# Gate tiles in 64-row matmuls, column sums by a DMA transpose, one fold matmul fewer, and a weight block loaded in two pieces

## The chip, the cores and the metric

One core of a Trainium2 chip. The time is the device time of one execution in microseconds (us), taken from several executions; all runs told of here are in the fast state. The executions of one kernel spread over some 0.6 to 0.9 us (before: 144.69 to 145.32 in one set of six, 144.84 to 145.74 in another of eleven), so effects of 0.1 us are read from traces, not from times. A ratio is the mean time of one kernel's fast runs over that of the other's fast runs in the same rounds, so it isn't quite the ratio of the medians that stand beside it.

In the profile lines PE is TensorE's matmuls, PEld its weight loads, DVE VectorE, ACT ScalarE, POOL GpSimd, SP SyncE (which here only issues DMAs: loads, stores and transposes). L708 is line 708 of that kernel's file, so the same code has other numbers in the changed kernel: L708 there is L709, L742 is L743, L972 is L973, L620 is L621, L679 is L680, L712 is L713. "Block 0" and "block 1" are the first 384 rows of the first two column blocks of `w1`; to "land" is to be complete in SBUF. The "first gate" and the "second gate" (nothing to do with the gate tiles) are two places where TensorE can be made to wait: before H4, for block 1, and near 15 us, for a PSUM bank.

## The reference

```python
xn = layernorm(A_x)                               # 2048 tokens, D = 448
q, k, v = split_heads(xn @ wqkv)                  # 16 heads of 28
pq, pk = phi(q), phi(k)                           # phi(t) = (t + 1 if t > 0 else exp(t)) + 1e-6
kv  = einsum("bhsd,bhse->bhde", pk, v)
z   = einsum("bhsd->bhd", pk)                     # column sums of pk over all tokens
num = einsum("bhqd,bhde->bhqe", pq, kv)
den = einsum("bhqd,bhd->bhq", pq, z) + 1e-6
s   = merge_heads(num / den) @ wo
h   = relu(xn @ w1 + b1) ** 2                     # F = 1792
g   = silu(h @ w2 + b2)
return A_x + s * g
```

## The kernel before

A small scheduler in the file takes a list of operations. TensorE's and SP's order is the order of the list; the order on VectorE, ScalarE and GpSimd is chosen by a simulation. All engines run their lists in order.

The first weight block and the first feed-forward units. `w1` comes in blocks of 512 columns: its first 384 rows (three chunks of 128) in one load, the last 64 rows in two small ones. H0 to H6 are the first seven units, done first for tiles 0 and 1 (part 0), then for tiles 2 and 3 (part 1):

```python
load_x(0, 1); load_x(1, 2); load_x(2, 4)          # SP
...                                               # small loads on ScalarE's queue
load_w1(0, "sp", "act")                           # block 0: 384 KB on SP
load_w1(1, "sp", "sp")                            # block 1: 384 KB and 2 x 32 KB on SP
load_x(4, 8)                                      # 448 KB
load_k("sp", w_qkv, A_wqkv, "wk", D, 2 * D)
...
for c in range(3):
    pe_part([H0[i] for i in range(4)], 0, (c,))   # 12 matmuls: chunk c of block 0 and of xT
pe_part([H0[i] for i in range(4, 6)], 0)          # H4, H5: 6 matmuls, need block 1
piece, evac = x_transpose0(2, [(0, 1, 2, 3)])     # 8 TensorE transposes of tiles 2, 3
...
pe_part([H0[6]], 0)
for c in range(3):
    pe_part([H0[i] for i in range(4)], 1, (c,))   # the "second halves": 12 matmuls
```

The pieces that the rest of the change touches:

```python
def gg(si):                                       # one gate tile: 14 matmuls of all 128 rows
    for fi in range(NF):
        e.matmul(ps(b)[:, 0:D], r2[:, fi, si*P:(si+1)*P], w_2[:, fi, :], start=(fi == 0), ...)
    ...                                           # VectorE adds b2
def z_cols():                                     # column sums: zb holds the sum over the token tiles
    for c in range(5):
        e.matmul(ps(b)[:, c:c+1], zb[:, k:k+P], ones[:, :], ...)
    ...                                           # VectorE multiplies by the head mask -> zsb
def fold_wo(c):                                   # c = 3: two matmuls of 64 columns each
    ...
def gg_part(si, lo, hi):                          # last tile, by halves: bias by a matmul, then 14
    e.matmul(ps(b)[:, 0:w], ident[:, :], b2b[:, lo:hi], start=True, stop=False)
    ...
```

The order after the first stage: the units of the second 512 tokens, the gate tiles 0 to 3, the units of the third and fourth 512 tokens, the token sums, `z_cols`, the denominators, the folds, the other gate tiles and the output.

## Time and profile before

| | |
|---|---|
| time | 144.98 us median (144.69 to 145.32, 6 runs) |
| TensorE busy | 138.0 of 143.1 us |
| VectorE, ScalarE, GpSimd busy | 65%, 54%, 23% |
| first matmul of H0 | 6.86 us |
| last matmul ends | 139.53 us |

TensorE sets the time from 6.9 us on. The chain's pieces are shown in the prediction.

### The profile page before, as it was taken

The page shows a single profiled execution, that of the slowest core. Times are in us where ns is not written, and L with a number is a line of the kernel's source. Part 1 is how long each engine was busy: PE and PEld are TensorE (multiplying, and loading weights), DVE is VectorE, ACT ScalarE, POOL GpSimd, SP SyncE. Part 2 cuts the span into 40 slices and gives each one's busy share as a digit, 9 for nine tenths or more (in the row PEclk, how much of TensorE's full clock was granted, in tenths as well). Part 3 has the DMA queues.
Part 4 walks back from the last instruction along what each step waited for, and adds up shares of the span by engine and source line. Part 5 has one row for each costly group of instructions (what it writes and reads, how often), then busy time and mean ns, then how long its engine had stood idle before and what let it go on. Part 6 is the DMA issues. An engine that isn't in the chain of part 4 may idle for free.

```text
span 143.1 us, 2830 instructions
## 1 busy us (share of the span) xinstructions
PE 138.0 (96%) x1114; PEld 72.4 (51%) x1114; DVE 92.5 (65%) x212; ACT 77.1 (54%) x148; POOL 32.7 (23%) x50
## 2 busy tenths in 40 slices
PE   7799999999999999999999999999999999999990
PEld 7685444444455444444444455546455554554590
DVE  5869879899997156768999760003511793575661
ACT  3617897988877088888879761178312131100120
POOL 2114026254000117300560000000000000399900
PEclk9999999999999999999999999999999999999999
DMA  3977899970452400000000000001499200024341
GB/s 80 315 247 201 173 240 337 338 170 0 41 111 55 92 0 5 0 0 0 5 0 0 5 0 0 0 0 23 124 174 179 39 0 5 0 75 149 116 144 33
DMA packets 17008, 12.43 MB, mean 87 GB/s; under 512 B 7844, under 2 KB 16100, under 8 KB 16996
## 3 DMA queue, kind: packets, MB, share of 16 engines
q1 hardware_dynamic: 16416, 11.28, 29.8%
q10 hardware_dynamic: 580, 0.97, 3.5%
q8 instruction: 9, 0.15, 0.4%
q14 instruction: 3, 0.02, 0.1%
HBM read 8.78 MB, written 1.90 MB: 75 GB/s over the span
## 4 chain that ended last, share of the span: by engine, by line
PE 93%; DVE 2%; DMA 1%; ACT 1%; issue 0%
PE pb L972 28%; PE pb L712 27%; PE pb L620 7%; PE pb L781 6%; PE pb L646 6%; PE pb L1041 6%; PE pb L708 3%; PE pb L994 2%; DMA x_tok<-in_A_x_dram 1%; PE pb L1114 1%; PE pb L660 1%; PE pb L787 1%; PE pb L857 1%; DVE st L462 1%; PE pb L809 1%; PE pb L879 1%
## 5 line engine op out<-in xcount | busy, mean ns | idle before, releaser
L972 PE MATMUL pb<-w,r 128*128 128x448 bf16 x210 | 40.7, 353 | 0.0
L712 PE MATMUL pb<-xT,w 64*128 64x512 bf16 (+1 forms) x291 | 38.1, 376 | 0.0
L679 ACT ACTIVATE r<-pb,b1f 128x512 bf16<-128x512 f32 x54 | 33.7, 691 | 6.8 <-PE pb L712 6.8
L972 PEld LDWEIGHTS pb<-w,r 128*128 128x128 bf16 x210 | 20.2, 98 | 19.5 <-issue 0.8
L1014 ACT ACTIVATE gbuf<-gbuf 128x448 bf16<-128x448 bf16 x15 | 8.1, 571 | 28.4 <-DVE gbuf L981 24.2
L1030 POOL TENSOR_TENSOR obuf<-obuf,x_tok 128x448 bf16<-128x448 bf16 x12 | 12.1, 1044 | 49.4 <-DVE obuf L1024 49.4
L981 DVE TENSOR_TENSOR gbuf<-pb,b2b 128x448 bf16<-128x448 f32 x15 | 9.3, 620 | 20.5 <-PE pb L972 20.5
L712 PEld LDWEIGHTS pb<-xT,w 64*128 64x128 bf16 (+1 forms) x291 | 14.3, 94 | 16.4
L693 DVE TENSOR_TENSOR r<-r 128x512 bf16<-128x512 bf16 x37 | 18.3, 523 | 2.9 <-ACT r L679 2.9
L630 POOL TENSOR_TENSOR zacc<-zacc,pk 128x448 f32<-128x448 f32 x13 | 14.4, 1107 | 22.8 <-DVE pk L610 22.3
L620 PE MATMUL pb<-w_qkv,xT 64*128 64x448 bf16 x112 | 13.2, 349 | 0.0
L1024 DVE TENSOR_TENSOR obuf<-pb,gbuf 128x448 bf16<-128x448 f32 (+1 forms) x17 | 9.3, 591 | 4.0 <-PE pb L1041 2.4
L598 ACT ACTIVATE pk<-pb 128x448 bf16<-128x448 f32 x16 | 7.8, 541 | 7.4 <-PE pb L620 7.4
L694 ACT ACTIVATE r<-r 128x512 bf16<-128x512 bf16 x19 | 11.2, 634 | 0.0
L646 PE MATMUL pb<-xT,w_qkv 64*128 64x512 bf16 x84 | 11.0, 376 | 0.0
L462 DVE BATCH_NORM_STATS2 st<-x_tok 128x6 f32<-128x448 bf16 x16 | 9.3, 615 | 1.7 <-DMA x_tok<-in_A_x_dram 1.7
L712 PE MATMUL pb<-xT,w_1r 64*128 64x512 bf16 x56 | 10.3, 377 | 0.0
L610 DVE SCALAR_TENSOR_TENSOR pk<-pb,pk 128x448 bf16<-128x448 f32 x16 | 9.9, 623 | 0.5
L781 PE MATMUL pb<-pk,xn 128*128 128x448 bf16 x48 | 9.4, 352 | 0.0
L603 DVE TENSOR_SCALAR pk<-pk 128x448 bf16<-128x448 bf16 x16 | 6.2, 392 | 4.4 <-ACT pk L598 4.4
L620 PEld LDWEIGHTS pb<-w_qkv,xT 64*128 64x128 bf16 x112 | 5.4, 94 | 6.1 <-issue 0.4
L610 DVE SCALAR_TENSOR_TENSOR pqT<-pb,pqT 128x512 bf16<-128x512 f32 x12 | 8.2, 689 | 0.3
(87 smaller groups left out, 123.8 us busy)
## 6 DMA issues: line engine op xcount, KB each, us to landing
out_dram<-obuf SPq DMA_DIRECT2D x15, 112.0 KB, 1.7
w<-in_B_w_dram SPq DMA_DIRECT2D x1, 1568.0 KB, 9.3
x_tok<-in_A_x_dram SPq DMA_DIRECT2D x3, 448.0 KB, 4.7
w<-in_B_w_dram SPq DMA_DIRECT2D x3, 384.0 KB, 4.5
w_qkv<-in_A_wqkv_dram SPq DMA_DIRECT2D x3, 336.0 KB, 5.5
pk<-rden_rows ACTq DMA_DIRECT2D x6, 112.0 KB
pk<-rden_rows SPq DMA_DIRECT2D x5, 112.0 KB
w_o<-in_A_wo_dram SPq DMA_DIRECT2D x1, 392.0 KB, 8.8
```

Source lines behind the costliest of these rows:

```text
L462: op = add("dve", lambda e, _: e.bn_stats(st6[:, si, :], x_tok[:, si, :]), [("x", si)], [("st", si)], 0.58)
L610: lambda e, _: e.scalar_tensor_tensor(out=slot, in0=ps(buf)[:, 0:n], scalar=1.0 + 1e-6, in1=slot, op0=ALU.add, op1=ALU.max),
L620: return e.matmul(ps(b)[:, 0:D], xT[rw, si, c, :], w_qkv[rw, c, D : 2 * D], start=start, stop=stop)
L630: lambda e, _: e.tensor_tensor(out=o[:, 0:D], in0=pk[:, 0, :] if i == 1 else zacc[:, :], in1=pk[:, i, :], op=ALU.add),
L646: return e.matmul(ps(b)[:, 0:512], w_qkv[rw, c, m * P : (m + 1) * P], xT[rw, 4 * g : 4 * g + 4, c, :], start=start, stop=stop,)
L679: rl = lambda e, _: e.activation(out=slot, in_=ps(b)[:, 0:512], func=AF.Relu, bias=b1f[:, fi : fi + 1])
L693: return e.tensor_tensor(out=slot, in0=slot, in1=slot, op=ALU.mult)
L694: return e.activation(out=slot, in_=slot, func=AF.Square)
L712: return e.matmul(ps(b)[:, 0:512], lhs, xT[rw, 4 * g : 4 * g + 4, c, :], start=start, stop=stop, skip_group_check=not full,)
L781: last = e.matmul(ps(b)[:, 0:D], xn[:, si, c * P : (c + 1) * P], pk[:, si, :], start=(si == 0), stop=(si == NT - 1),)
L972: last = e.matmul(ps(b)[:, 0:D], r2[:, fi, si * P : (si + 1) * P], w_2[:, fi, :], start=(fi == 0), stop=(fi == NF - 1),)
L1030: lambda e, _: e.tensor_tensor(out=ob, in0=ob, in1=x_tok[:, si, lo:hi], op=ALU.add),
```

## The change

Its intent: take slots and changes of array form off TensorE, and let it start on the first chunk of `w1` before the others are there. The core of the diff, with cuts marked:

```diff
+            for c0, c1 in ((0, 1), (1, 3)) if p == 0 else ((0, 3),):      # load_w1
+                dma(eng, w_1[:, c0:c1, lo:hi], B_w1[c0*P : c1*P, lo:hi]..., [("w1", p, 0, c) for c in range(c0, c1)], ...)
...
-            need = {("xTp", 2 * part, k) for k in cs} | {u[1][0] for u in us}
+            need = {("xTp", 2 * part, k) for k in cs} | {u[1][0] + (k,) for u in us for k in cs}
...
         def z_cols():
-            ... five matmuls with a column of ones, one multiply
+            add("sp", lambda e, _: e.dma_start_transpose(zbT[:, :, :], zb[:, :]), ...)
+            add("dve", lambda e, _: e.tensor_reduce(out=zcol[:, :], in_=zbT[:, :, :], op=ALU.add, axis=X), ...)
+            ... two multiplies by the mask
...
         def fold_wo(c):
-                for o in range(1 if c < 3 else 2): ... 64-column halves for c = 3
+                for h in hs: e.matmul(ps(b)[:, 0:D], kvm[0:PD, h, c*P:(c+1)*P], w_o[0:PD, h, :], ...)
...
+        def gg4(t):                       # four gate tiles; two 64-row matmuls at a time
+            for i, pair in enumerate(((t, t+2), (t+1, t+3), (t+2, t), (t+3, t+1))):
+                for fi in range(NF):
+                    for h in (0, 1):
+                        e.matmul(ps(bufs[pair[h]])[:, 0:D], r2[half[h], fi, ...], w_2[half[h], fi, :], ...)
...
-        gg(0)
-        gg(1)
-        gg(2)
-        gg(3)
+        gg4(0)
...
-        gg_part(15, 0, 224)
+        gg_part(15, 0, 224, False)        # bias by VectorE instead of a matmul
```

The warm-up matmuls also read a constant instead of a tile that VectorE clears first, `kvm` is 512 wide, and the scheduler's estimate for the denominators is 0.88 us instead of 0.22.

More of the change, by code (lines that the diff above doesn't have):

```diff
@@ L312, in bass_recurrent_scan__linear_attn_block__dense_activation_squared_relu__prompt_kernel @@
         zmask = sb("zmask", [P, 5, 32], f32)
-        ones = sb("ones", [P, 1], bf)
-        wz = sb("wz", [P, P], bf)
+        wz = nc.const_aps.tensor(1.0, [P, P], bf)
         rsp = nc.dram_tensor("rden_rows", [NH, 2, 1024], bf)
@@ L336, in bass_recurrent_scan__linear_attn_block__dense_activation_squared_relu__prompt_kernel @@
         zb = sb("zb", [P, 512], bf)
+        zbT = sb("zbT", [P, 4, P], bf)
+        zcol = sb("zcol", [P, 4], f32)
         at = sb("at", [P, 4, D], bf)
@@ L339, in bass_recurrent_scan__linear_attn_block__dense_activation_squared_relu__prompt_kernel @@
         r2 = sb("r2", [P, NF, S], bf)
-        kvm = sb("kvm", [P, 4, D], bf)
+        kvm = sb("kvm", [P, 4, 512], bf)
         msb = at
@@ L373, in vset @@
             add("dve", lambda e, _: e.memset(ap, val), [name] if again else [], [name], dur)
-        vset(wz[:, :], 0.0, "wz")
-        pr.ops[-1].prio = -1e6
         vset(hmask[:, :], 1.0, "hmask", dur=0.15)
@@ L379, in bass_recurrent_scan__linear_attn_block__dense_activation_squared_relu__prompt_kernel @@
         vset(kvm[:, :, :], 0.0, "kvm", dur=1.0)
-        pool(lambda e, _: e.memset(ones[:, :], 1.0), ["ones"], dur=0.1)
         pool(lambda e, _: e.memset(eps6[:, :], 1e-6), ["eps6"], dur=0.1)
@@ L433, in load_w1 @@
             m = (hi - lo) // 2
-            dma(
-                eng, w_1[:, :, lo:hi], B_w1[0:384, lo:hi].rearrange("(c p) j -> p c j", p=P), [("w1", p, 0)],
-                768 * (hi - lo), reads,
-            )
+            for c0, c1 in ((0, 1), (1, 3)) if p == 0 else ((0, 3),):
+                dma(
+                    eng, w_1[:, c0:c1, lo:hi], B_w1[c0 * P : c1 * P, lo:hi].rearrange("(c p) j -> p c j", p=P),
+                    [("w1", p, 0, c) for c in range(c0, c1)], (c1 - c0) * 256 * (hi - lo), reads,
+                )
             load_w1r(p, eng2)
         w1names = lambda p: [("w1", p, i) for i in range(3)]
+        for p in range(4):
+            pr.alias(("w1", p, 0), [("w1", p, 0, c) for c in range(3)])
         load_x(0, 1)
@@ L816, in fold_wv @@
             add("pe", f, [("at", c) for c in range(4)] + wnames("wv"), [b], 16 * 0.057)
-            kd = free_ap(kvm[0:PD, 0:1, 0:PD], [[D + PD, 4], [1, PD]])
+            kd = free_ap(kvm[0:PD, 0:1, 0:PD], [[512 + PD, 4], [1, PD]])
             add(
@@ L825, in fold_wv @@
             )
+            add(
+                "dve", lambda e, _: e.tensor_copy(kvm[0:PD, 3, D:512], kvm[0:PD, 3, 384:D]), ["kvd"], ["kve"], 0.12
+            )
         def z_cols():
-            b = Buf("Z")
-            def f(e, _):
-                last = None
-                for c in range(5):
-                    k = min(c, 3) * P
-                    last = e.matmul(
-                        ps(b)[:, c : c + 1], zb[:, k : k + P], ones[:, :], start=(c == 0), stop=True,
-                        skip_group_check=True,
-                    )
-                return last
-            add("pe", f, ["zb", "zbd", "ones"], [b], 0.35)
-            z = lambda: free_ap(ps(b)[:, 0:5], [[1, 5], [0, 32]])
-            add(
-                "dve", lambda e, _: e.tensor_tensor(out=zsb[:, :, :], in0=z(), in1=zmask[:, :, :], op=ALU.mult),
-                [b, "zmask"], ["zsb"], 0.25,
-            )
+            add(
+                "sp", lambda e, _: e.dma_start_transpose(zbT[:, :, :], zb[:, :]),
+                ["zb", "zbd"], ["zbT"], 1.25, nbytes=P * 512 * 3,
+            ).fixed = 2.0
+            add(
+                "dve",
+                lambda e, _: e.tensor_reduce(
+                    out=zcol[:, :], in_=zbT[:, :, :], op=ALU.add, axis=mybir.AxisListType.X
+                ),
+                ["zbT"], ["zcol"], 0.6,
+            )
+            for i, n in ((0, 4), (4, 1)):
+                z = free_ap(zcol[:, min(i, 3) : min(i, 3) + n], [[1, n], [0, 32]])
+                add(
+                    "dve",
+                    lambda e, _, i=i, n=n, z=z: e.tensor_tensor(
+                        out=zsb[:, i : i + n, :], in0=z, in1=zmask[:, i : i + n, :], op=ALU.mult
+                    ),
+                    ["zcol", "zmask"], [("zsb", i)], 0.2,
+                )
         def fold_wo(c):
@@ L852, in f @@
                 last = None
-                for o in range(1 if c < 3 else 2):
-                    dst = ps(b)[:, 0:D] if c < 3 else ps(b)[64 * o : 64 * o + 64, 0:D]
-                    wd = P if c < 3 else 64
-                    for h in hs:
-                        last = e.matmul(
-                            dst, kvm[0:PD, h, c * P : c * P + wd], w_o[0:PD, h, :], start=(h == hs[0]),
-                            stop=(h == hs[-1]),
-                        )
+                for h in hs:
+                    lhs = kvm[0:PD, h, c * P : (c + 1) * P]
+                    last = e.matmul(ps(b)[:, 0:D], lhs, w_o[0:PD, h, :], start=(h == hs[0]), stop=(h == hs[-1]))
                 return last
-            add("pe", f, ["kvd", "kvm", "wo"], [b], 0.19 * len(hs) * (2 if c == 3 else 1))
+            add("pe", f, ["kvd", "kvm", "wo"] + (["kve"] if c == 3 else []), [b], 0.19 * len(hs))
             def ev(e, eng):
@@ L894, in den @@
                 "pe", f,
-                ["zsb"] + [("pq", g, c) for g in range(NG) for c in range(3)]
+                [("zsb", 0), ("zsb", 4)] + [("pq", g, c) for g in range(NG) for c in range(3)]
                 + [("pqx", u) for u in (0, 1)],
-                [denb], 0.22,
+                [denb], 0.88,
             ).mode = "col32"
@@ L985, in gg, with gg_bias, f, gg_part @@
             )
-        def gg_part(si, lo, hi):
+        def gg_bias(si, b):
+            add(
+                "dve",
+                lambda e, _: e.tensor_tensor(
+                    out=gbuf[:, si % NGB, :], in0=ps(b)[:, 0:D], in1=b2b[:, :], op=ALU.add
+                ),
+                [b, "b2b"], [("g", si % NGB)], 0.624,
+            )
+        def gg4(t):
+            half = (slice(0, 64), slice(64, 128))
+            bufs = {si: Buf("G") for si in range(t, t + 4)}
+            ops = []
+            for i, pair in enumerate(((t, t + 2), (t + 1, t + 3), (t + 2, t), (t + 3, t + 1))):
+                def f(e, _, pair=pair, i=i):
+                    last = None
+                    for fi in range(NF):
+                        for h in (0, 1):
+                            si = pair[h]
+                            last = e.matmul(
+                                ps(bufs[si])[:, 0:D], r2[half[h], fi, si * P : (si + 1) * P], w_2[half[h], fi, :],
+                                start=(i < 2 and fi == 0), stop=(i >= 2 and fi == NF - 1),
+                            )
+                    return last
+                banks = [bufs[si] for si in pair]
+                rd = [("r2", t // 4, fi) for fi in range(NF)] + ["w2"]
+                op = add("pe", f, rd + (banks if i >= 2 else []), banks, NF * MM(D))
+                op.mode = "row64"
+                ops.append(op)
+                if i >= 2:
+                    op.sync = ops[-3]
+                    for si in pair:
+                        gg_bias(si, bufs[si])
+        def gg_part(si, lo, hi, bias):
             b = Buf("G")
             w = hi - lo
+            gs = gbuf[:, si % NGB, lo:hi]
             def f(e, _):
-                last = e.matmul(ps(b)[:, 0:w], ident[:, :], b2b[:, lo:hi], start=True, stop=False)
+                last = e.matmul(ps(b)[:, 0:w], ident[:, :], b2b[:, lo:hi], start=True, stop=False) if bias else None
                 for fi in range(NF):
                     last = e.matmul(
-                        ps(b)[:, 0:w], r2[:, fi, si * P : (si + 1) * P], w_2[:, fi, lo:hi], start=False,
-                        stop=(fi == NF - 1),
+                        ps(b)[:, 0:w], r2[:, fi, si * P : (si + 1) * P], w_2[:, fi, lo:hi],
+                        start=(fi == 0 and not bias), stop=(fi == NF - 1),
                     )
@@ L1000, in gg_part @@
             rd = [("r2", si // 4, fi) for fi in range(NF)] + ["w2", "b2b", "ident"]
-            add("pe", f, rd, [b], (NF + 1) * max(MM(w), 0.098))
-            add(
-                "act",
-                lambda e, _: e.activation(out=gbuf[:, si % NGB, lo:hi], in_=ps(b)[:, 0:w], func=AF.Silu),
-                [b, "acts"], [("gh", lo)] + ([("g", si % NGB)] if lo == 0 else []), 0.2 + 0.00084 * w,
+            add("pe", f, rd, [b], (NF + bias) * max(MM(w), 0.098))
+            wr = [("gh", lo)] + ([("g", si % NGB)] if lo == 0 else [])
+            if not bias:
+                add(
+                    "dve",
+                    lambda e, _: e.tensor_tensor(out=gs, in0=ps(b)[:, 0:w], in1=b2b[:, lo:hi], op=ALU.add),
+                    [b, "b2b"], wr, 0.1 + w * 0.00118,
+                )
+            add(
+                "act", lambda e, _: e.activation(out=gs, in_=ps(b)[:, 0:w] if bias else gs, func=AF.Silu),
+                [b if bias else ("gh", lo), "acts"], wr, 0.2 + 0.00084 * w,
             )
@@ L1128, in f @@
                 for _i in range(n):
-                    last = e.matmul(ps(wb)[:, 0:P], wz[:, :], wz[:, :], start=True, stop=True)
+                    last = e.matmul(ps(wb)[:, 0:P], wz, wz, start=True, stop=True)
                 return last
-            add("pe", f, ["wz", *after], [wb], n * cost)
+            add("pe", f, list(after), [wb], n * cost)
         def quads(what):
@@ L1232, in bass_recurrent_scan__linear_attn_block__dense_activation_squared_relu__prompt_kernel @@
             zsum(i)
+        z_cols()
         quads("Q2.0 H3.4 Q2.1 H3.6 Q2.2 H3.5 Q3.0 H3.7 Q3.1 H3.12 Q3.2 H3.13")
@@ L1239, in bass_recurrent_scan__linear_attn_block__dense_activation_squared_relu__prompt_kernel @@
         token_sum(1)
-        z_cols()
         token_sum(2)
@@ L1272, in bass_recurrent_scan__linear_attn_block__dense_activation_squared_relu__prompt_kernel @@
         s_main(us[2], 2)
-        gg_part(15, 0, 224)
+        gg_part(15, 0, 224, False)
         s_main(us[3], 3, True, 0, 224)
-        gg_part(15, 224, D)
+        gg_part(15, 224, D, True)
         s_main(us[3], 4, True, 224, D)
```

## The prediction

> **What bounds the kernel now.** I read first the busy times and the 40 slices, then the chain that ended last in order of time, then the list of waits, the timeline of the first 16 us and the issue-to-landing times of the first loads. TensorE is busy 138.0 us of a 143.1 us span, at full granted clock in every slice, and the chain of waits is 93% TensorE:
>
> ```profile
> PE 138.0 (96%) x1114; PEld 72.4 (51%) x1114; DVE 92.5 (65%) x212; ACT 77.1 (54%) x148; POOL 32.7 (23%) x50
> PEclk9999999999999999999999999999999999999999
> PE 93%; DVE 2%; DMA 1%; ACT 1%; issue 0%
> ```
>
> From the first tile's feed-forward matmuls (about 6.9 us) to the last matmul (139.5 us) TensorE almost never stops. So no engine beside it has to be made faster; only slots on TensorE, stalls on it, and the short head and tail count. In the chain I therefore looked for pieces that last longer than their number of slots times the pace. Columns: start us, duration us, what:
>
> ```profile
> 5.95 0.66 ACT xT L758 x2
> 6.61 0.19 ACT vep L471
> 6.79 0.07 issue
> 6.86 2.12 PE pb L708 x18
> ...
> 37.55 10.70 PE pb L972 x56
> 48.25 0.86 PE pb L620 x8
> 49.11 0.86 PE pb L712 x8
> 49.97 0.57 PE pb L620 x6
> 50.54 0.65 PE pb L712 x6
> 51.19 0.76 PE pb L620 x8
> ...
> 90.36 0.10 PE pb L834 x5
> 90.47 3.05 PE pb L781 x16
> ...
> 98.07 2.65 PE pb L972 x14
> 100.72 1.45 PE pb L857 x8
> 102.17 18.64 PE pb L972 x98
> ...
> 136.35 0.10 PE pb L992
> ```
>
> What to see: a gate tile of 14 full matmuls of 448 columns that follows other full matmuls takes 2.65 us, 0.189 us each. Eight 64-row matmuls of the same width (L620), two at a time on the array halves, take 0.76 us, again 0.189 us per pair: both forms have the same pace. But where the form changes, the piece is about 0.10 us longer: 56 gate matmuls take 10.70 instead of 4 x 2.65 = 10.60, and the first L620 group after them takes 0.86 where the next one takes 0.76. The same surcharge stands at the output fold (L857) and after it, and at other changes that stay.
>
> **What the Trainium skill says.** "TensorEngine Tiling (Array Packing)", Tiling Modes, Key Properties: changing the tiling mode, as against the tile, drains the TensorE. The trace agrees in kind, and gives the size that the page lacks: about 0.10 us. The same page, Gotcha 1, says row tiles write different PSUM banks and raise the pressure on them; the 64-row groups of this kernel already use four banks at a time without a TensorE wait. "TensorE: Matmul & The Clock Gate", Part 1: warm matmuls start every N / 2.4 GHz plus about 2.5 ns; for 448 columns that is 0.189 us, just what is seen. "DMA: Bandwidth & Descriptors", Rules for kernel authors: issue a DMA early and wait late, so its fixed cost overlaps. The six DMA transposes in this trace take 3.1 to 5.1 us from issue to landing, median 3.4, well over that page's fit of some 2 us fixed, and only an early issue would hide one.
>
> **The change part by part.**
>
> *First four gate tiles in 64-row form.* 112 half-height matmuls, paired, are 56 slots at 0.189 us: 10.6 us, no arithmetic saved. Before them and after them stand 64-row groups (L712 and L646 before, L620 after), so two mode changes vanish: 10.70 - 10.60 and 0.86 - 0.76, **-0.20 us**. The price is that four banks are held together, and that biases come off in two pairs of 0.62 us each at the end instead of one by one. The stage needs two banks at the start, two more after 2.65 us, and four others remain for the next group; the last pair is freed some 1.3 us after the end, when the next group of four is still running (it lasts 2.85 us). I count no stall.
>
> *Column sums by DMA transpose.* Five one-column matmuls and their 0.10 us leave the path, and the token sum after them takes 3.05 instead of 16 x 0.189 = 3.03: **-0.12 us**. In exchange there are one DMA transpose, a VectorE reduction over 512 elements and two small multiplies. The sums come from zb, which POOL finishes at 74.1 + 0.24 = 74.3 us; with 3.4 us to land (the median above) the transpose is there at about 77.8. The reduction is some 0.6 us (estimate: the 512-element tensor operations from PSUM in this trace take 0.69), the multiplies 0.2 each. The denominators start on TensorE at 93.5 us. VectorE is full until about 80 us but idle from 84.7 to 90.5 us, so even at the lowest priority the result is there 6 to 8 us early. SyncE has nothing else between its last load and the store of denominators at 95.9 us. Hidden.
>
> *Last fold chunk in one matmul.* L857 has six full matmuls and two 64-column ones that run together: 7 slots x 0.189 = 1.325 us, measured 1.45, thus 0.12 for the change of form; the 98 gate matmuls after it take 18.64 instead of 98 x 0.1893 = 18.55, 0.09 for changing back. Afterwards there are again seven slots, all full: **-0.21 us**. The added VectorE copy of 64 columns (0.1 to 0.2 us) comes after the mask multiply that ends at 98.7 us and is wanted only at about 101.3. The wider clearing of kvm (0.81 us for 896 words, so about 0.93 for 1024) is before the first x arrives at 2.9 us, and the clearing of wz goes.
>
> *Bias of the first half of the last tile.* One matmul of 224 columns leaves TensorE (L992 at 136.35): **-0.10 us**. VectorE gets an addition of about 0.37 us and ScalarE works on SBUF in place. That half now leaves about 0.3 us later: addition to about 138.1, activation 138.5, product 138.9, x added 139.2. VectorE is wanted for the second half at 139.9, so the chain at the very end doesn't see it.
>
> *First w1 rows apart, and an earlier warm-up.* TensorE idles 0.62 us before L708. The profile names ACT vep, but L708's first group needs only xT chunk 0 (ready at 5.95 + 0.33 = 6.28) and w1; the load of w1 was issued at 2.20 and took 4.5 us, landing at 6.7. So the DMA is what is waited for. The first 128 KB alone should land near 5.9 (estimate: the previous x load landed at about 5.5, and 128 KB at the 330 GB/s of the slices there take 0.4 us), so chunk 0's four matmuls can start at 6.33 and save 0.43 us. I don't believe all of it. The twelve matmuls over the first half of H0..H3 are followed by H4 and H5, which need the second w1 block: issued at 2.86, 5.1 us to landing, so 7.96, and its queue is limited by bytes, which do not become fewer. With the 0.13 us that passed between the first block's landing and its first weight load, H4 starts at 8.08 at the earliest, against 8.16 now (6.86 + 12 x 0.108). So **-0.1 us**, and most of the stall moves from before chunk 0 to before H4. The warm-up starts about 0.2 us earlier because it doesn't wait for wz, but the transposes after it wait for xn at 5.57 all the same: nothing.
>
> Sum: 0.20 + 0.12 + 0.21 + 0.10 + 0.10 = 0.73 us. 144.86 - 0.73 = 144.13, say **144.1 us**.
>
> **Rivals.** (1) *The head pays in full.* If the second w1 block has reserve that I don't see, 0.43 instead of 0.1 is won: total 1.06, 143.8 us. For it speaks that TensorE showed no stall at H4 before; against it, that the load lands only 0.2 us before use. (2) *A new wait in the gate stage.* If four banks held together or the two late pairs of biases hold up the K2 and H2 groups, or VectorE's extra 0.6 us there pushes bank releases, some 0.2 to 0.6 us come back: 144.3 to 144.7. For it: VectorE and ScalarE are 80 to 100% busy around 50 to 80 us. Against: no TensorE wait in the list after 10 us, and idle VectorE and ScalarE during the gate tiles themselves. (3) *The column-sum work lands in VectorE's fullest stretch.* Engines run in order, so if the reduction stands in the queue before the transpose has landed, VectorE stalls for up to a microsecond near 77 us, where it is 95% busy, and keeps query banks. TensorE could lose up to 0.5 us: 144.6. Against: the schedule gives it low priority, since it is wanted at 93 us. (4) *The extra SP issue delays everything after it* by the 0.6 us that one issue takes; x tiles 4 to 7 and K's weights would come later. Against: these queues are limited by bytes until 9.5 us, and TensorE needs K's weights only at 13.7.
>
> **Range and chances.** The certain part (mode changes, six removed slots or short matmuls) is 0.63 us; the head adds 0 to 0.45, the rivals can take 0.6 away. The three runs before spread 0.33 us. Eight in ten: 143.7 to 144.7. A verdict of faster needs 2.9 us, four times all I can find; slower needs a stall of over 3.5 us that nothing in the trace prepares. So 0.98 for the middle.
>
> **What would show it.** In the changed profile: the gate tiles at about 37 us as 112 matmuls in 10.6 us with no 0.10 us surcharge on either side; no one-column matmuls, and the denominators not waiting for VectorE or DMA; the fold in 1.33 us; one bias matmul instead of two; L708's first four matmuls near 6.3 us, then a gap before the chunks of w1 or before H4. I am wrong if a TensorE wait on a bank, on the transposed sums, or on w1's later rows over 0.3 us appears, or if the surcharges stay where the form no longer changes.

## More of the kernel before

One more view matters later: how fast the loads come in while TensorE waits for its first weights. It is the table of busy times by stretch; the last two columns are the mean busy share of the 16 DMA engines and GB/s (kernel before):

```profile
4.75:6.25 1.50, 1.38 (x17) 0.82 (x14) 1.15 (x4) 0.84 (x5) 0.47 (x2) 1.00 0.94 314
```

The engines are busy (0.94) and move 314 GB/s between 4.75 and 6.25 us.

## The result, and the profile after

144.76 us median (144.25 to 145.08, 6 runs) against 144.98; ratio 0.9979, 95% interval 0.9956 to 1.0003. The time lies just above the stated range, and of the 0.73 us only 0.22 (by the medians) or 0.30 (by the ratio) was won; since the interval holds 1, the times alone don't even show that much.

The chain of the changed kernel, the same pieces as shown of before (start us, duration us, what):

```profile
3.50 4.96 DMA w<-in_B_w_dram
8.45 0.05 issue
8.50 0.83 PE pb L709 x6
9.33 0.46 PE pb L743 x8
...
37.88 10.59 PE pb L1008 x112
48.48 0.76 PE pb L621 x8
...
84.33 9.19 PE pb L782 x48
...
100.72 1.32 PE pb L861 x7
102.05 18.54 PE pb L973 x98
...
136.12 1.34 PE pb L1032 x14
```

Everything behind 37 us went as foretold. The gate tiles take 10.59 us with no surcharge, and the group after them 0.76 instead of 0.86; the token sums are one unbroken 9.19 us where before had 6.16 + 0.10 + 3.05; the fold takes 1.32 instead of 1.45 and the 98 matmuls behind it 18.54 instead of 18.64; the bias matmul is gone. But the second group of transposes starts at 9.33 us, and before it stood at 8.99: the head lost 0.34 us. The chain now leads from H4's matmuls (L709 x6) to a load of `w1`. The timeline of TensorE there (start us, duration us, engine, line, operation, and in brackets the idle time before and what ended it):

```profile
6.28 0.61 PE L709 MATMUL pb<-xT,w 128*128 128x256 bf16 x4
7.17 1.03 PE L709 MATMUL pb<-xT,w 128*128 128x256 bf16 x8 [0.28 <-DMA w<-in_B_w_dram]
8.50 0.83 PE L709 MATMUL pb<-xT,w 128*128 128x256 bf16 x6 [0.30 <-DMA w<-in_B_w_dram]
```

The first chunk's four matmuls do start at 6.28. Then TensorE waits for the other rows of block 0, and before H4 for block 1: issued at 3.50, it took 4.96 us and landed at 8.45, where before had it at 8.0. In the stretch between 4.75 and 6.25 us the loads of the changed kernel move much less:

```profile
4.75:6.25 1.50, 1.22 (x14) 0.83 (x13) 1.15 (x4) 0.81 (x5) 0.47 (x2) 1.00 0.89 207
```

207 GB/s instead of 314. Over 1.5 us that is 160 KB fewer, or, at before's 314 GB/s, some 0.5 us (an estimate from these two rates); block 1 came some 0.5 us late. That the two agree is partly luck: over all traces the rate doesn't give the lateness (see the end of the experiments).

The balance over the two traces: gate tiles -0.21, column sums -0.12, fold -0.23, bias -0.10, head +0.34, in all -0.32 us. The last matmul ends at 139.20 instead of 139.53. (The two profiled runs differ by 0.78 us in time, 144.36 and 145.14; the part beyond 0.33 lies after the last matmul or outside the span, and the medians don't show it.)

### The profile page after: what moved, and what is told of

It is laid out like the page before. It is cut to its first block, busy times and chain, and to the rows that moved or that the text cites. A ratio compares the mean times of both kernels' runs of the same rounds, so it can differ in the third digit from the quotient of the medians.

```text
span 142.4 us, 2932 instructions
## 1 busy us (share of the span) xinstructions
PE 137.7 (97%) x1163; PEld 72.2 (51%) x1163; DVE 92.5 (65%) x217; ACT 76.2 (54%) x146; POOL 32.9 (23%) x49
## 4 chain that ended last, share of the span: by engine, by line
PE 92%; DMA 3%; SPq 2%; DVE 1%; issue 0%; ACT 0%
PE pb L713 27%; PE pb L973 21%; PE pb L621 7%; PE pb L1008 7%; PE pb L782 6%; PE pb L647 6%; PE pb L1085 6%; DMA w<-in_B_w_dram 3%; PE pb L709 2%; PE pb L1032 2%; SPq L400 2%; PE pb L1158 1%; PE pb L661 1%; PE pb L788 1%; PE pb L861 1%; PE pb L810 1%
## 5 line engine op out<-in xcount | busy, mean ns | idle before, releaser
L973 PE MATMUL pb<-w,r 128*128 128x448 bf16 x154 | 30.0, 353 | 0.0
L973 PEld LDWEIGHTS pb<-w,r 128*128 128x128 bf16 x154 | 14.8, 98 | 14.1 <-DVE obuf L1068 0.4
L982 DVE TENSOR_TENSOR gbuf<-pb,b2b 128x448 bf16<-128x448 f32 x11 | 6.8, 623 | 23.0 <-PE pb L973 23.0
L694 DVE TENSOR_TENSOR r<-r 128x512 bf16<-128x512 bf16 x39 | 17.8, 496 | 2.1 <-ACT r L680 2.0
L1008 PE MATMUL pb<-w,r 64*128 64x448 bf16 x112 | 10.8, 349 | 0.0
L695 ACT ACTIVATE r<-r 128x512 bf16<-128x512 bf16 x17 | 10.2, 634 | 0.0
```

What stands on the lines that cost most here:

```text
L694: return e.tensor_tensor(out=slot, in0=slot, in1=slot, op=ALU.mult)
L695: return e.activation(out=slot, in_=slot, func=AF.Square)
L973: last = e.matmul(ps(b)[:, 0:D], r2[:, fi, si * P : (si + 1) * P], w_2[:, fi, :], start=(fi == 0), stop=(fi == NF - 1),)
L1008: last = e.matmul(ps(bufs[si])[:, 0:D], r2[half[h], fi, si * P : (si + 1) * P], w_2[half[h], fi, :], start=(i < 2 and fi == 0), stop=(i >= ...
```

## The experiments

Theories at the start. A: the extra issue on SP (0.6 us) makes block 1's own issue, and so its landing, late. B: the late landing is chance. C: it is the two pieces themselves, whoever issues them; later D (each further load costs its own time) and E (a small piece that comes first moves slowly). Rivals F (x tiles 4 to 7 are a second gate) and G (what is in flight behind a load delays it) came up on the way.

For each trace the table has when block 1 landed (its issue plus its time to landing), GB/s between 4.75 and 6.25 us, when SP issued x tiles 4 to 7 and when they landed, the start of the second group of transposes in the timeline, the end of the last matmul, and the ratio to before.

| run | block 0 | block 1 landed | GB/s | x tiles issued, landed | transposes | last matmul | ratio (95%) |
|---|---|---|---|---|---|---|---|
| before | one load | 8.0 | 314 | 4.80, 10.1 | 8.82 | 139.53 | |
| changed | 128 + 256 KB | 8.5 | 207 | 5.27, 10.8 | 9.16 | 139.20 | 0.9979 (0.9956 to 1.0003) |
| c4_after_again | the same | 8.3 | 223 | 5.26, 11.0 | 9.05 | 139.47 | 0.9969 (0.9945 to 0.9993) |
| a1_unsplit | one load | 8.0 | 340 | 4.80, 9.5 | 8.88 | 138.92 | 0.9951 (0.9923 to 0.9980) |
| b1_split_only | 128 + 256 | 8.6 | 218 | 5.25, 11.3 | 9.31 | 140.41 | 1.0048 (1.0019 to 1.0076) |
| b2_tiny_issue | one load, then 2 KB | 8.2 | 308 | 5.32, 10.9 | 8.87 | 139.97 | 1.0013 (0.9979 to 1.0046) |
| a2_rows_on_act | 128 + 256, two queues | 8.6 | 178 | 4.75, 10.0 | 10.86 | 141.22 | 1.0061 (1.0020 to 1.0103) |
| c1_two_then_one | 256 + 128 | 8.0 | 272 | 5.26, 11.1 | 8.69 | 139.53 | 0.9962 (0.9936 to 0.9987) |
| c2_transpose_first | 128 + 256 | 8.3 | 209 | 5.26, 10.9 | 7.93 | 138.95 | 0.9942 (0.9910 to 0.9974) |
| c3_unsplit_h4_first | one load | 7.9 | 308 | 4.80, 9.3 | 8.42 | 138.87 | 0.9949 (0.9927 to 0.9972) |
| d1_gates_apart | one load | 8.2 | 315 | 4.78, 9.6 | 8.94 | 140.28 | 1.0040 (1.0018 to 1.0063) |
| d2_after_x_early | 128 + 256 | 9.9 | 190 | 4.01, 11.2 | 10.62 | 140.66 | 1.0049 (1.0033 to 1.0066) |
| d3_two_one_x_early | 256 + 128 | 9.0 | 227 | 4.01, 10.4 | 9.71 | 139.76 | 0.9988 (0.9959 to 1.0017) |
| d4_h4_first_lead1 | one load | 8.3 | 333 | 4.82, 9.8 | 10.38 | 140.52 | 0.9943 (0.9924 to 0.9962) |
| e1_hold_behind | 128 + 256 | 8.3 | 174 | 8.28, 11.6 | 8.97 | 139.25 | 1.0011 (0.9963 to 1.0059) |
| e2_before_x_early | one load | 8.2 | 274 | 3.54, 9.5 | 8.86 | 139.56 | 1.0011 (0.9995 to 1.0028) |

### One load again: a1_unsplit

```diff
-            for c0, c1 in ((0, 1), (1, 3)) if p == 0 else ((0, 3),):
+            for c0, c1 in ((0, 3),):
```

> The changed kernel with the first w1 block in one load again, the rest of the change kept; all engines but SP have the same order as in the changed kernel. Theory A (the extra issue on SP delays the second w1 block): its issue is back at 2.86 us, it lands at 7.95, H4 isn't held up, the second group of transposes (8 on TensorE) starts near 9.0 instead of 9.33, and the time falls by 0.33 us against the changed kernel: 144.3 to 144.4 where before is 144.98, ratio to before 0.9955. Rival B (the split is harmless and the late landing was chance of one profile): ratio stays near 0.998, transposes near 9.3 again or anywhere between 9.0 and 9.4.

144.44 us median, 145.13 for before beside it. The head of its chain is that of the kernel before:

```profile
6.91 2.12 PE pb L709 x18
9.04 0.46 PE pb L743 x8
```

340 GB/s flow between 4.75 and 6.25 us, and the whole of the other parts' gain arrives: 0.9951 is 0.71 us, where the pieces of the chain add up to 0.66. In the traces, then, the split is what gave the gain back: the last matmul ends at 138.92 here, at 139.20 and 139.47 in the two traces of the changed kernel. The times alone don't separate a1 from the changed kernel (0.9979 and 0.9969, with overlapping intervals); b1 tries the split by itself.

### The split alone: b1_split_only

The kernel before with the two loads and the finer waits of the change, nothing else.

> The kernel before with only the split of the first w1 load and its finer waits; other engines in the same order as before. Theory A: issue of the second block 0.64 us later, landing 0.5 later at about 8.45, transposes at 9.3 instead of 8.99: slower by 0.3 us, ratio 1.002. Rival B (chance): ratio 1.000 or lower. My own prediction, were it right, would give 0.9993.

Slower by 0.7 us (by the interval, 0.3 to 1.1), twice what theory A and the changed kernel's trace say. Block 1 landed at 8.6 and the transposes came 0.49 us later, but the chain of waits then went another way (start us, duration us, what):

```profile
5.25 6.05 DMA x_tok<-in_A_x_dram
11.30 0.02 issue
11.32 2.20 DVE st L462 x4
...
14.38 1.16 ACT r L679 x2
...
15.59 1.04 PE pb L712 x8
```

What to see: x tiles 4 to 7 landed at 11.3 us. VectorE's statistics of these tiles wait for them, ScalarE's next step in its list waits for the statistics, and behind that step stand two bias-and-relu operations (L679) that have to empty PSUM banks. TensorE needs such a bank at 15.59: the piece takes 1.04 us instead of 0.86, and an idle 0.2 us stands before it. This is a second gate, and one that my prediction had named and dismissed (rival 4). c4_after_again, the changed kernel in another execution, shows it too, where the changed kernel's first trace did not.

### An issue without bytes: b2_tiny_issue

```diff
-        load_w1(0, "sp", "act")
+        load_w1(0, "sp", "act"), dma("sp", tiny[:, :], A_x[0][0:P, 0:8], ["tiny"], P * 16)
```

> The kernel before with one more load on SP between the first and the second w1 block, of 2 KB into an unused tile: an issue without bytes. Theory A: the issue alone (0.4 to 0.6 us) delays the second block to 8.3 to 8.5, H4 waits, transposes 0.2 to 0.35 us later, ratio 1.001 to 1.002. Rival C (the pieces or bytes matter, not the issue): second block at 7.95, nothing changes, ratio 1.000.

Inconclusive in time (1.0013, the interval holds 1). In the trace block 1 was issued at 3.55 instead of 2.86 and yet landed at 8.2, only some 0.2 us late; the rate stayed at 308 GB/s. TensorE waited 0.28 us at H4, but it had started early enough that the transposes moved by 0.05 us only. So for block 1 an issue by itself costs little. But x tiles 4 to 7, issued at 5.32 instead of 4.80, landed at 10.9 instead of 10.1, and the second gate then cost this trace nearly all of the 0.44 us by which its last matmul is late (timeline of TensorE):

```profile
15.14 0.82 PE L712 MATMUL pb<-xT,w 64*128 64x512 bf16 x6 [0.22 <-ACT r L679]
```

### The other rows from another queue: a2_rows_on_act

```diff
                 dma(
-                    eng, w_1[:, c0:c1, lo:hi], ...
+                    "act" if c0 else eng, w_1[:, c0:c1, lo:hi], ...     # after ScalarE's small loads
```

> The changed kernel with the split kept, but the later rows (256 KB) issued from the ScalarE queue after its small loads, at about 2.7 us, so that SP issues the second w1 block at 2.84 as before. Theory A: second block lands near 7.95 and H4 starts near 8.1; chunk 0 starts at 6.3; transposes at about 8.7 to 8.9; 0.4 to 0.5 us less than the changed kernel, ratio to before 0.9945. Rival C (two pieces of the block are slower to move than one, whoever issues them): second block lands at 8.3 or later as in the changed kernel, transposes at 9.2 or later, ratio 0.998.

A miss for theory A. SP issued block 1 as early as before did, and it still landed at 8.6; the rate was 178 GB/s. (The x tiles, though, also issued as early as before did, landed at 10.0, as there.) The other rows of block 0, issued at 2.73 from ScalarE's queue, landed only at 7.93, so TensorE idled 1.01 us. And then this (timeline of TensorE, and the stretch behind it; the column before the last two is the granted clock):

```profile
7.98 2.23 PE L709 MATMUL pb<-xT,w 128*128 128x256 bf16 x10 [1.01 <-DMA w<-in_B_w_dram]
```

```profile
8.00:9.50 1.50, 1.50 (x8) 1.12 (x9) 0.39 (x2) 0.00 (x0) 0.00 (x0) 0.53 1.03 355
```

Over the stretch the granted clock was 0.53: these matmuls ran at half the pace until after 11 us. The six runs show it as two groups, three at 146.7 to 146.8 us with a mean clock of 0.987 or 0.988, and three at 144.9 to 145.8 with 1.0. The slow group loses over 1 us more than the other. It wasn't in any theory, and that the stall brought it on isn't shown: only one of these runs has a trace, and in d2, below, a longer wait of 1.9 us left the clock at 1.0.

### Split the other way: c1_two_then_one

```diff
-            for c0, c1 in ((0, 1), (1, 3)) if p == 0 else ((0, 3),):
+            for c0, c1 in ((0, 2), (2, 3)) if p == 0 else ((0, 3),):
```

> The changed kernel with the first w1 block split the other way: 256 KB first, 128 KB second; the other engines' order is unchanged. Theory D (every further load in that queue costs its own time, whatever its size): block complete and second block as late as in the changed kernel, 8.45, ratio 0.998. Theory E (the piece whose turn comes soonest after its issue moves slowly, about 190 GB/s, because little is queued ahead of it; a large first piece gives the rest time): pieces land near 6.4 and 6.8, second block at 8.0 to 8.15, transposes at 9.0, ratio 0.995.

The first gate opened in time, as theory E has it: block 1 at 8.0, the transposes at 8.69, 0.13 us before those of the kernel before. E's reason isn't shown by that: it had the first piece near 6.4, and it landed at 5.7. The rate is 272 GB/s, between the other two groups. But x tiles 4 to 7 landed at 11.1, and the second gate took all of it back (timeline of TensorE):

```profile
15.37 0.82 PE L713 MATMUL pb<-xT,w 64*128 64x512 bf16 x6 [0.62 <-ACT r L680]
```

The last matmul of that trace ends at 139.53, as before's does, although 0.66 us of other work is gone from TensorE. In time the run is at 0.9962, no different from the changed kernel beside it (0.9969).

### Nobody waits for the late block: c2_transpose_first and c4_after_again

c4_after_again is the changed kernel itself, on the same chip as c1, c2 and c3.

> The changed kernel itself, beside the others on one chip. Before's runs say that the issue order on SP alone (Theory A) is not the cause, because with the later rows issued from ScalarE's queue the second block still landed at 8.5 us. What stands: the second w1 block lands late whenever the first is in two pieces (8.45, 8.5, 8.6 us in three traces, against 7.96 and 8.06 in one piece). If so: second block lands at 8.3 to 8.7 again, second group of transposes at 9.2 to 9.5, ratio to before 0.996 to 0.999. If chance: it may land near 8.0 here, and the ratio may reach 0.995.

The lateness is no chance: 8.3 us, 223 GB/s, and a wait of 0.28 us at H4. Ratio 0.9969. Its last matmul ends only 0.06 us before before's: of the 0.66 us, the first gate took 0.23 (transposes at 9.05 instead of 8.82) and the second 0.38 (an idle 0.20 near 15 us, and a group of 1.04 instead of 0.86).

c2 keeps the split, and moves H4 and H5 behind the transposes of tiles 2 and 3:

```diff
-        pe_part([H0[i] for i in range(4, 6)], 0)
         piece, evac = x_transpose0(2, [(0, 1, 2, 3)])
...
-        pe_part([H0[6]], 0)
+        pe_part([H0[i] for i in range(4, 7)], 0)
```

> The changed kernel, split kept, with TensorE's order altered so that the late second block isn't waited for: the transposes of tiles 2 and 3 come before H4 and H5. If the wait at H4 is what gave the gain back, transposes start near 8.45 instead of 9.33, the second halves (12 matmuls after the evacuation) near 9.86 instead of 10.16, and 0.3 us are won although the load lands as late as ever: ratio near 0.9955. If the wait at H4 isn't what counts (because something later, such as x tiles 4 to 7, sets the pace anyway), the ratio stays near 0.998.

The chain of c2 at the transposes and behind them:

```profile
8.48 0.40 PE pb L743 x4
8.88 2.29 PE pb L709 x21
```

The block lands as late as ever (8.3), but TensorE does the transposes in the meantime and goes straight through 21 matmuls. The last matmul ends at 138.95, 0.25 us before the changed kernel's first trace and 0.52 before c4's. 144.14 us median against 144.65 for c4 on the same chip, four runs and six, with intervals that overlap. In the traces 0.35 of the 0.52 us stand already at the first group of `w_1r` matmuls (11.11 against 11.46): the wait at H4 is what held the gain at the first gate. (The scheduler also gave ScalarE and VectorE a slightly different order there. At the second gate c2's group of eight matmuls at 14.78 took 1.04 instead of 0.86 us, some 0.2 us lost; c4 lost 0.4 there, which is the rest of the difference from c4.)

### A version meant to beat both: c3_unsplit_h4_first, then d4_h4_first_lead1

a1 with TensorE's order H4, transposes, H5, H6:

> A version meant to beat both: first w1 block in one load, and TensorE's order H4, transposes, H5, H6, so that H5 and H6 fill the evacuation. Expected second halves at 9.65 instead of 9.87 (one load) or 10.16 (changed kernel): 0.2 us less than with one load alone, ratio to before 0.9935 to 0.994. If ScalarE's in-order queue holds banks until x tiles 4 to 7 are in (a wait of TensorE near 15 us appears), part of it is lost and the ratio is 0.995.

144.32 us median, ratio 0.9949. The transposes came at 8.42, the second halves 0.2 us earlier than a1's, but the group at 14.71 took 1.03 us instead of 0.86, and the last matmul ends 0.05 us before a1's. (Here x tiles 4 to 7 had landed at 9.3, so late tiles are not the only thing that can make this group longer.) Then the statistics' priority was cut (`lead=3` to `lead=1`), which changes ScalarE's order there:

> A version meant to beat both: first block in one load, H4 then transposes then H5 and H6, and the scheduler's lead for the statistics of tiles 4 to 7 cut from 3 to 1 us, which puts one bias-and-relu ahead of ScalarE's second statistics step. With the order H4, transposes, H5, H6 alone the second halves started at 9.64 but the group at 14.71 took 1.03 instead of 0.86 us. Expected: that surcharge goes, the last matmuls end 0.15 to 0.2 us earlier than with that order alone, ratio to before 0.9935. If ScalarE's queue isn't what holds the bank, nothing changes: 0.995.

144.29 us median, ratio 0.9943 (0.9924 to 0.9962); seven runs, six from 143.92 to 144.45 and the profiled one at 146.08. (The ratio fits the six, whose mean gives 0.9946; all seven give 0.9965.) In the profiled one an early x load landed at 4.14 us, where the other traces have it at 3.4 to 4.0, and the first fifteen matmuls took 3.12 us, about 0.21 each, twice the warm pace; so the trace can't tell whether the surcharge at 15 us went in the usual executions. That stays open.

### Is the 0.10 us the change of form? d1_gates_apart

The kernel before with gate tiles 1 to 3 moved apart, each between two groups of 64-row matmuls: eight changes of form instead of two.

> The kernel before with gate tiles 1 to 3 moved apart, one each after a group of four of the next stage, so that TensorE changes between 64-row and full form eight times there instead of twice. If a change of form costs 0.10 us each time, as the chain of the kernel before suggests, each of the four tiles takes 2.75 us instead of 2.65 and the group after each is 0.10 us longer: 0.6 us more in all, ratio 1.004. If the 0.10 us belonged to the stage (a bank or a wait) and not to the change of form, the pieces show no surcharge and the ratio is 1.000.

145.61 us median against 144.87, ratio 1.0040 (1.0018 to 1.0063), that is 0.58 us. The chain shows where:

```profile
37.66 2.76 PE pb L972 x14
40.41 0.86 PE pb L620 x8
...
43.35 2.75 PE pb L972 x14
46.11 0.86 PE pb L620 x8
```

Every gate tile takes 2.75 instead of 2.65 us, wherever it stands, and the two groups of eight that stand alone behind one take 0.10 us more. The surcharge belongs to the change of form.

### What lies behind the block: d2, d3, e1, e2

First, x tiles 4 to 7 ahead of block 1's two small loads, in the changed kernel (d2) and with the pieces in the other order (d3):

```diff
-            load_w1r(p, eng2)
+            load_w1r(p, eng2) if p != 1 else None
...
-        load_x(4, 8)
+        load_x(4, 8), load_w1r(1, "sp")
```

> The changed kernel with x tiles 4 to 7 issued ahead of the second block's two small loads; the other engines' order is the same. Theory F (a second gate: x tiles 4 to 7 land at 10.8 to 11.1 us because of the extra load, VectorE's statistics and ScalarE's in-order queue then hold PSUM banks until TensorE waits near 15 us): these tiles land at 10 us or before, VectorE doesn't wait for them, no wait near 15 us; the wait for the second w1 block stays. Against the changed kernel (0.2 us of such a wait in one of its two traces) a gain of 0.1 to 0.3 us, ratio to before 0.996. If the order of these loads doesn't matter: ratio 0.997 to 0.998 and x tiles land near 10.8 again.

> First block split as 256 then 128 KB, and x tiles 4 to 7 early. With the two pieces in that order the second block came in time, but TensorE waited 0.6 us for ScalarE at 15.4 us, where the chain led back to x tiles 4 to 7 landing at 11.1. Theory F: that wait shrinks to 0.2 us or nothing, the group of 8 matmuls there starts near 14.8 instead of 15.37, ratio to before 0.993 to 0.9945. If the second gate isn't these tiles, the wait stays at 0.6 and the ratio at 0.996.

Both missed. d2: 145.72 us, ratio 1.0049 (1.0033 to 1.0066), and the chain says why:

```profile
3.50 6.41 DMA w<-in_B_w_dram
9.90 0.04 issue
9.95 0.83 PE pb L709 x6
```

Block 1, issued at 3.50 as in the changed kernel, landed at 9.9, and the x tiles, issued 1.3 us earlier than there, only at 11.2. d3: ratio 0.9988 (0.9959 to 1.0017), block 1 at 9.0; the tiles landed at 10.4, and the wait near 15 us was gone, but TensorE also came there later. So a load issued *behind* another delays it; theory F could not be tried in this way, since the order that brings the tiles early makes block 1 late. It made theory G, which two more runs tried. e1: the changed kernel, with SP waiting for block 1 before it issues x tiles 4 to 7; nothing large is behind the block. e2: the kernel before, in one piece, with the x tiles right behind block 1.

> The changed kernel, split and all, but SP issues x tiles 4 to 7 and K's weights only when the second w1 block has landed, so nothing large is in flight behind that block. Theory G (loads in one queue share the engines, and what is issued behind a load delays it): the second block, issued at 3.5 as before, lands at 8.0 or earlier instead of 8.3 to 8.45, and TensorE's wait at H4 is gone or under 0.1 us. Theory D (the extra load itself, or its late issue, costs the time): it still lands at 8.3 to 8.45. The whole kernel will be slower in either case, since x tiles 4 to 7 come after 11 us; the time decides nothing here.

> The kernel before, first block in one load, with x tiles 4 to 7 issued ahead of the second block's two small loads; other engines in the same order. Theory G: the second block, issued at 2.86 as before, lands at 8.8 or later instead of 7.96, because 448 KB are in flight right behind it; TensorE waits at H4 for over 0.5 us; ratio 1.004 or more. Theory D (only splitting, or a late issue of the block itself, delays it): it lands near 8.0, x tiles come earlier, ratio 1.000 or below.

Theory G falls as the main cause. In e1 block 1 still lands at 8.3 and the rate is 174 GB/s, though nothing large is behind it. In e2 the block lands at 8.2, inside the range of the other one-load traces (7.9 to 8.3), the rate is 274 GB/s, and the time is unclear (1.0011, 0.9995 to 1.0028). So, one trace each, what is right behind a block cost nothing that shows when the loads before it came in one piece, 1.0 us when they came as 256 + 128 KB (d3), and 1.5 us as 128 + 256 KB (d2). (e1's time, 1.0011 with 0.9963 to 1.0059 from two runs, decides nothing, as said there.)

What stands over all traces: with block 0 in one load the rate between 4.75 and 6.25 us was 274 to 340 GB/s in seven traces (before, a1, b2, c3, d1, d4, e2), with 128 + 256 KB it was 174 to 223 in seven (changed, c4, c2, b1, a2, d2, e1), with 256 + 128 KB it was 272 and 227 (c1, d3). Block 1 landed at 7.9 to 8.3 us with one load and at 8.3 to 8.6 with 128 + 256 KB (without d2): 8.1 against 8.4 in the mean, with ranges that touch. The rate of a trace doesn't give the lateness: e1, with 174 GB/s, had block 1 at 8.3, and b1, with 218, at 8.6. Why two pieces of the same bytes are moved more slowly stays open: it isn't the issue time of SP alone (a2, b2), nor the traffic behind (e1). The same tables give a hint: the DMA engines' mean busy share in that stretch was 0.94 to 1.02 with one load and 0.71 to 0.89 with 128 + 256 KB, so they stood still for part of it; but in the changed kernel's own trace it was 0.89 against 0.94, for a third fewer bytes, so there they were mostly busy and slower.

The second gate follows another pattern, and here what theory A said of block 1 holds. Where the order of the loads was kept, x tiles 4 to 7 landed at 9.3 to 10.1 us when SP issued them at 4.75 to 4.82 (before, a1, a2, c3, d1, d4), and at 10.8 to 11.3 when it issued them at 5.25 to 5.32 (changed, c4, c2, c1, b1, b2). a2 has the pieces without the extra issue on SP, and b2 the extra issue without the pieces: so what makes these tiles late is the extra issue.

## Why the prediction was wrong, point by point

- **Gate tiles, column sums, fold, bias: right.** Foretold 0.20, 0.12, 0.21 and 0.10 us, found 0.21, 0.12, 0.23 and 0.10. d1 confirmed the surcharge by doing it six times more.
- **Hidden costs: right, with one size off.** The transpose of the column sums took 4.2 us to landing, not the median 3.4, so VectorE stood still for 1.44 us in its full stretch. That is the stall of rival 3, against which the prediction had the low priority of this work:

```profile
78.67 0.69 DVE L838 TENSOR_REDUCE zcol<-zbT 128x4 f32<-128x512 bf16 x1 [1.44 <-DMA zbT<-zb]
```

  TensorE never waited on it, nor on a bank in the gate stage (rival 2), nor on the later bias.
- **The head: wrong, and it is the step that failed.** The prediction said of block 1: "its queue is limited by bytes, which do not become fewer", and had H4 start at 8.08 for a gain of 0.1 us. The bytes were the same, but the rate was not: 207 instead of 314 GB/s just then. Block 1 landed at 8.45, H4 started at 8.50, and the head lost 0.34 us instead of winning 0.1. That the split makes block 1 late is shown (b1; a2 and b2 against the issue alone); why is not. Chunk 0 was right (6.28 against 6.33), and so was the remark that the stall moves to before H4; its size was not.
- **Rival 4: it came true for the x tiles.** The prediction dismissed it with "these queues are limited by bytes until 9.5 us". In the changed kernel SP issued x tiles 4 to 7 at 5.27 instead of 4.80 us, and they landed at 10.8 instead of 10.1. In b1, b2, c1, c2 and c4, where they landed at 10.9 to 11.3, TensorE lost 0.2 to 0.8 us near 15 us; in the changed kernel's first trace, at 10.8, it lost nothing, so there the loss of the head is all block 1.
- **The range.** It took 0.6 us off the sum for rivals, which gave 144.7; the median was 144.76. By the prediction's own terms the upper end was too low: 144.86 - 0.63 + 0.6 is 144.83. Its start, 144.86, was the median of three runs, and six gave 144.98. And it let the head add 0 to 0.45 us but never take any; that is the term with the wrong sign. With block 0 in one load (a1) the same change is at 144.44 and 0.9951: the sum without the head, 0.63 us, fits (0.71 by the ratio, 0.66 by the trace).

Best versions: a1, c2, c3 and d4 stand at 0.9942 to 0.9951, each faster than before beyond its interval. Their intervals overlap with each other and with the changed kernel's own on c4's chip (0.9969), so they can't be ranked; beside the changed kernel on one chip stood only c2 and c3 (144.14 and 144.32 against 144.65).

## What to carry to other kernels

Read the rate of the loads in the stretch that matters before assuming that a queue is limited by bytes; a split that lets the first consumer start earlier can make everything behind it later, and the first thing to check is who waits for the *next* load. An extra issue, even one of 2 KB (b2), also delays what stands behind it in the same list. When several small gains are bundled with one risky one, test the risky one by undoing it alone: here it gave back half of what the others had won. Where a load is late anyway, giving the engine other ready work first (c2) did as well, within the noise, as getting the load earlier.

## What the Trainium skill lacked or had wrong

- "TensorEngine Tiling (Array Packing)" says that changing the tiling mode drains the engine, and gives no size: here 0.10 us for each change between 64-row and full matmuls (d1: six more of them, 0.58 us).
- "DMA: Bandwidth & Descriptors", Rules for kernel authors, calls small loads (under 64 KB) mostly overhead; neither it nor another page says what splitting a larger one costs the loads around it: with 384 KB as 128 + 256 KB the rate was 174 to 223 GB/s instead of 274 to 340, and the next block landed at 8.3 to 8.6 us instead of 7.9 to 8.3.
- The same page, Queues, rings and completion order, says that completion isn't first in, first out, and gives no size for how much a load is delayed by one issued behind it: with 448 KB issued right behind block 1 it landed at 9.9 us instead of 8.3 to 8.6 in the split kernel (d2), and at 8.2 in the unsplit one (e2), where other traces have 7.9 to 8.3.
- "TensorE: Matmul & The Clock Gate", Part 1, puts the return to half clock after an idle window of about 3.4 us. In a2's trace the longest idle time was 1.0 us, with TensorE busy for half of the 3 us before 8.0, and the granted clock was 0.53 and then 0.50 from 8.0 to 11.0 us (two more of its six runs have nearly the same mean clock, 0.987 against 0.988); a wait of 1.9 us in d2 left it at 1.0.
- "Advanced Engine Details and Errata", X-Bar Transpose (TRN2), says transposing DMAs are as fast as others. With no other DMA of SP in flight, the 128 x 512 bf16 transpose between SBUF tiles took 4.2 us to landing; loads of x of 112 KB took 2.1 to 2.4.
